# A fixed instruction order for the first two thirds of an attention and expert kernel, fp32 projections on quarters of the array, and VectorE steps over two PSUM banks

## The chip, the core and the metric

The kernel runs on one core of a Trainium2 chip. The metric is the device time of one execution in microseconds (us); lower is better. The engines are TensorE (PE in the profile, its weight loads PEld), VectorE (DVE), ScalarE (ACT), GpSimd (POOL) and SyncE (SP), whose queue issues most transfers. Each engine runs its own instructions in order and waits for the others by semaphores.

## What is computed

Three parts in a row, all in fp32 accuracy:

```python
# linear attention: 2 batches, 8 heads, 576 tokens, head size 64, 128 random features
phi(x): h = (x*scale) @ omega.T - |x*scale|^2/2;  h -= max(h);  exp(h) / sqrt(128)
kv  = sum over tokens of phi(k) v^T;  z = sum of phi(k)
x   = phi(q) kv / (phi(q) z + 1e-6)                      # 1152 tokens x 512
# gated linear part
x   = (((x @ w1) * (x @ w2)) @ w3) @ w_out               # 512 -> 1024 -> 1024 -> 512
# routed experts: 8 experts, one per token, capacity 288
e   = argmax(x @ w_gate);  gate = softmax(x @ w_gate)[e]
y   = relu(x @ e1[e]) @ e2[e];  out = gate * y for tokens within the capacity
```

The weights w1, w2, w3 and w_out come as float64.

## The kernel before

*Precision.* Most products split each fp32 operand into a high part (`F32R`, fp32 rounded for one fast pass) and a low part, and multiply in three passes, `PASS = ((0,0),(0,1),(1,0))`: high x high, high x low, low x high.

*Attention.* Tokens go in 9 tiles of 128, for k (`k0`..`k8`) and q (`q0`..`q8`). A tile is loaded as 128 partitions (two heads of 64 features) x 4 head pairs x 128 tokens. `split` (L195) casts it to high on ScalarE and takes the low part on GpSimd, or on VectorE for k0 and k2. `phi` (L202) projects, for each of two groups `g` of four heads, by 6 matmuls of 256 columns against `om_hl`, a block-diagonal omega; then VectorE takes the maximum per head (L212), and either VectorE subtracts it and ScalarE takes one exponential of 512 (L215, L216), or ScalarE takes four exponentials of 128 with the maximum as bias (L219); `SUBK` and `SUBQ` say which. `kv_add` (L238) accumulates phi(k) v into two PSUM banks, on half arrays of 64 columns. For q, `q_tr` (L221) transposes, `num` (L254) multiplies by kv, and VectorE divides (L267 to L269), `x_tr` (L272) transposes the result and splits it (L286, L287).

*Hidden layer.* `ab_mm(f, c, w)` (L425) is 12 matmuls of 288 columns for feature block f (8 of 128), token quarter c (4 of 288) and w1 or w2: 64 such groups. The product of the two goes to `g_t[f]` on VectorE (L448) or, for f 4 to 6, on GpSimd (L446). `turn` (L402) transposes 32 x 32 blocks on VectorE (L405), and `store` writes them to the table `gd` in DRAM from where the experts' tokens are gathered.

*Weights.* A block of 512 KB of float64 is loaded (L322, L344), VectorE builds fp32 in three steps on the integer words (L325 to L327, L350 to L355), ScalarE casts the high part and GpSimd takes the low part (L330/L331, L360/L364). 40 blocks: 8 each of w1, w2 and w_out, and 16 of w3. `W(f)` (L465) is w3 x w_out, 24 matmuls of 512 columns. `gate_t`, `gate_u` and `logits` (L487 to L513) make w3 w_out w_gate and the gate logits.

*Order.* The front part, up to the bar in `PLAN` (L49), is written in program order, with the order of each engine but TensorE left to the tile framework. From the bar on, `tick` (L133) hands out the pending steps of weight blocks and transposes between the matmul groups, at most one step an engine, and `keep_order` (L164) fixes the order found on VectorE, ScalarE, GpSimd and SP; `in_order(nc.tensor)` fixes TensorE's from the start. The closing part, with routing, gathers and experts, is ordered by the string `END` (L58), and the last 12 `ab_mm` groups stand in it. PSUM's eight banks are three rings: `pa` of 4, `pm` of 2, `px` of 2.

Of the kernel before, what the change touches and what calls it, by code (L numbers as in the profile page):

```python
# [28 lines left out]
AHEAD = 4  # L29
# [4 lines left out]
DVE_LOW = ("k0", "k2")  # L34

SUBK = [(0, 1), (), (0, 1), (0, 1), (), (), (), (), ()]
SUBQ = [(1,), (0, 1), (0, 1), (1,), (), (1,), (1,), (), (1,)]

KV_AT = {2: (0,), 4: (1, 2), 6: (3, 4), 8: (5, 6), 10: (7, 8)}


STEP = "PTtpANXa"

POOL_AB = [(f, b) for f in range(4, 7) for b in range(2)]

PLAN = (  # L49
# [3 lines left out]
)  # L53


# [6 lines left out]
def attention_moe_kernel(ctx: ExitStack, tc: tile.TileContext, qT, kT, v, om, w1, w2, w3, wo, wg, e1, e2, cap, out):  # L62
# [13 lines left out]
    psa = ctx.enter_context(tc.tile_pool(name="psa", bufs=4, space=bass.MemoryType.PSUM))  # L76
    psm = ctx.enter_context(tc.tile_pool(name="psm", bufs=2, space=bass.MemoryType.PSUM))

    psx = ctx.enter_context(tc.tile_pool(name="psx", bufs=2, space=bass.MemoryType.PSUM))

    def px(nm):
        return psx.tile([128, 512], F32, tag="px", name=nm)
# [28 lines left out]
    todo, active, out_of, done_of, LIM = [], [], {"wr": 0, "u": 0, "W": 0}, {}, {"wr": 2, "u": 2, "W": 2}  # L111
    late, hold, leave = [False], [False], set()
# [57 lines left out]

    zeros = wt("W", [128, 4 * (D + 1)], F16, "zeros")
    nc.gpsimd.memset(zeros, 0.0)
    om_sb = u([128, 2 * M], F32, "om_sb")
    nc.sync.dma_start(out=om_sb, in_=om)
    om_hl = wt("W", [128, 2, 2 * M], F32R, "om_hl")

    A.mul(out=om_hl[:, 0], in_=om_sb, mul=SCALE)
    V.scalar_tensor_tensor(out=om_hl[:, 1], in0=om_sb, scalar=SCALE, in1=om_hl[:, 0].bitcast(F32), op0=ALU.mult, op1=ALU.subtract)
# [4 lines left out]
    kt, qt, vt, kp, qp, qpT, kvz, kvp, xs, xhl = {}, {}, {}, {}, {}, {}, {}, {}, {}, {}  # L183

    def load(dst, src, i, nm):
        dst[i] = kq([128, 4, 128], F32, f"{nm}{i}")
        nc.sync.dma_start(out=dst[i], in_=src[i].rearrange("p (k t) -> p k t", k=4))

    def load_v(i):
        vt[i] = u([128, H, D + 1], F32, f"v{i}")  # L190
        nc.sync.dma_start(out=vt[i], in_=v[i * 128:(i + 1) * 128, :].rearrange("p (h d) -> p h d", d=D + 1))

    PASS = ((0, 0), (0, 1), (1, 0))

# [892 lines left out]
```

## Time and profile before

| | |
|---|---|
| time, median of 3 runs | 336.76 us (336.29 to 336.81) |
| the profiled execution's own time | 335.43 us |
| its span, first to last instruction | 333.6 us |
| TensorE busy | 319.7 us, 96%, 2963 matmuls |
| VectorE busy | 220.7 us, 66% |
| ScalarE busy | 145.9 us, 44% |
| GpSimd busy | 135.5 us, 41% |
| moved by the transfers | 47.77 MB |

The attention fills the first 63 us or so, the hidden layer and the W products run up to the routing near 215 us, and gathers and experts follow. Busy time of TensorE is a sum over stretches in which at least one matmul is under way; the end of a matmul is modelled, so its start is the surer number. In a timeline, a row with xN stands for N instructions in a row, its length from the first start to the last end.

### The profile page before, as it was taken

To read this page: it belongs to the slowest core of one execution; us is meant where nothing else is said; L and a number is where in the kernel's file an instruction comes from. 1 tells how busy PE (TensorE), PEld (TensorE's weight loads), DVE (VectorE), ACT (ScalarE), POOL (GpSimd) and SP (SyncE) were. 2 spreads that over 40 slices of the span, in tenths; PEclk is the share of its full clock that TensorE was granted. 3 is DMA by queue.
4 is the path that set the end of the run, shared out by engine and by line. 5 is a ranking of instruction groups with operands and counts; after the bars stand their busy time and mean duration, and the time that the engine had idled before them with its cause. 6 is when DMAs were issued, how large, how long until landed. Compare 5 with 4: busy or idle time off the path is not lost. (4 is left out here: it accounts for less than half of the span.)

```text
span 333.6 us, 7487 instructions
## 1 busy us (share of the span) xinstructions
PE 319.7 (96%) x2963; PEld 295.1 (88%) x2963; DVE 220.7 (66%) x426; ACT 145.9 (44%) x347; POOL 135.5 (41%) x118
## 2 busy tenths in 40 slices
PE   8899989999999999999999998999999999999991
PEld 6799979999998898897788896899799999899991
DVE  2979999999998944935889864380696714416110
ACT  4899898843322233243334243211553625327100
POOL 3736930133344243453575556025071633247021
PEclk9999999999999999999999999999999999999997
DMA  7986110143454728994244430994789772350011
GB/s 242 398 327 178 55 59 2 63 128 129 140 178 135 259 112 184 215 184 83 73 131 157 147 126 3 317 109 122 274 179 131 250 231 65 104 159 1 3 30 46
DMA packets 25148, 47.77 MB, mean 143 GB/s; under 512 B 3116, under 2 KB 12460, under 8 KB 25110
## 3 DMA queue, kind: packets, MB, share of 16 engines
q1 hardware_dynamic: 16950, 40.18, 39.1%
q10 hardware_dynamic: 7104, 3.54, 7.8%
q0 software_dynamic: 1056, 3.54, 3.7%
q8 instruction: 25, 0.41, 0.5%
q14 instruction: 13, 0.11, 0.1%
HBM read 38.98 MB, written 8.27 MB: 142 GB/s over the span
## 5 line engine op out<-in xcount | busy, mean ns | idle before, releaser
L433 PE MATMUL ab<-xh,w_hl 128*128 128x288 f32 x512 | 107.9, 299 | 0.8 <-ACT a_sb L437 0.6
L433 PEld LDWEIGHTS ab<-xh,w_hl 128*128 128x128 f32 x512 | 83.5, 188 | 4.0 <-issue 1.9
L433 PE MATMUL ab<-xl,w_hl 128*128 128x288 f32 x256 | 75.5, 295 | 0.0
L433 PEld LDWEIGHTS ab<-xl,w_hl 128*128 128x128 f32 x256 | 48.1, 188 | 0.0
L472 PE MATMUL W<-wo_hl,w_hl 128*128 128x512 f32 x192 | 46.3, 396 | 0.0
L472 PEld LDWEIGHTS W<-wo_hl,w_hl 128*128 128x128 f32 x192 | 35.5, 188 | 7.6
L364 POOL TENSOR_TENSOR w_hl<-w_f,w_hl 128x512 fp32r<-128x512 f32 x22 | 30.2, 1382 | 11.7 <-ACT w_hl L360 9.5
L405 DVE STREAM_TRANSPOSE gs<-g 128x576 f32<-128x576 f32 x16 | 19.7, 1232 | 15.3 <-POOL g L446 15.2
L360 ACT CAST w_hl<-w_f 128x512 fp32r<-128x512 f32 x22 | 13.7, 625 | 35.6 <-DVE w_f L355 32.1
L841 PE MATMUL r_x2p<-r_xc,W 128*128 128x288 f32 x192 | 26.8, 297 | 0.2 <-DVE r_yo L875 0.2
L350 DVE TENSOR_SCALAR w_f<-w_raw 128x512 uint32<-128x512 uint32 x22 | 17.8, 809 | 13.7 <-POOL w_hl L364 12.9
L841 PEld LDWEIGHTS r_x2p<-r_xc,W 128*128 128x128 f32 x192 | 25.8, 188 | 0.5 <-DVE r_yo L875 0.4
L331 POOL TENSOR_TENSOR wo_hl<-wo_f,wo_hl 128x512 fp32r<-128x512 f32 x8 | 11.2, 1406 | 34.1 <-PE xT L276 18.4
L480 POOL TENSOR_TENSOR W<-W_raw,W 128x512 fp32r<-128x512 f32 x8 | 10.8, 1351 | 30.9 <-ACT u_all L504 23.7
L331 POOL TENSOR_TENSOR w_hl<-w_f,w_hl 128x512 fp32r<-128x512 f32 x10 | 14.0, 1401 | 22.4 <-ACT w_hl L330 22.4
L437 ACT COPY a_sb<-ab 128x288 f32<-128x288 f32 x32 | 12.7, 398 | 21.3 <-PE ab L433 20.7
L355 DVE SCALAR_TENSOR_TENSOR w_f<-w_raw,w_f 128x512 uint32<-128x512 uint32 x22 | 20.5, 932 | 0.6
L351 DVE SCALAR_TENSOR_TENSOR w_f<-w_raw,w_f 128x512 uint32<-128x512 uint32 x22 | 18.7, 848 | 0.8
L446 POOL TENSOR_TENSOR g<-a_sb,b_sb 128x288 f32<-128x288 f32 x12 | 10.7, 888 | 18.0 <-ACT b_sb L445 15.6
L761 POOL TENSOR_TENSOR r_e_00l<-r_e_0r,r_e_00h 128x512 fp32r<-128x512 f32 x4 | 6.1, 1514 | 29.0 <-ACT r_e_00h L757 21.1
L210 PE MATMUL pjk<-om_hl,k_hl 128*128 128x256 f32 x108 | 15.2, 291 | 1.7 <-DVE kp L215 1.6
L448 DVE TENSOR_TENSOR g<-a_sb,ab 128x288 f32<-128x288 f32 x20 | 8.9, 447 | 11.9 <-PE ab L433 11.9
(233 smaller groups left out, 681.7 us busy)
## 6 DMA issues: line engine op xcount, KB each, us to landing
w_raw<-in_w SPq DMA_DIRECT2D x32, 512.0 KB, 3.6
wo_raw<-in_wo SPq DMA_DIRECT2D x8, 512.0 KB, 3.9
gd<-gs ACTq DMA_DIRECT2D x12, 288.0 KB, 7.9
v<-in_v SPq DMA_DIRECT2D x9, 260.0 KB, 5.7
k<-in_kT SPq DMA_DIRECT2D x9, 256.0 KB, 4.5
q<-in_qT SPq DMA_DIRECT2D x9, 256.0 KB, 7.1
out<-zero SPq DMA_DIRECT2D x1, 2304.0 KB
r_e_0r<-in_e SPq DMA_DIRECT2D x4, 512.0 KB
```

The source lines that it names most:

```text
L210: nc.tensor.matmul(out=ps[:, r * 256:(r + 1) * 256], lhsT=t[:, s, k * 128:(k + 1) * 128], rhs=om_hl[:, w], start=(n == 0), stop=(n == 2))
L331: nc.gpsimd.tensor_tensor(out=hl[1], in0=f.bitcast(F32), in1=hl[0].bitcast(F32), op=ALU.subtract)
L350: V.tensor_scalar(out=f, in0=r[:, :, 1], scalar1=3, scalar2=0x3FFFFFF8, op0=ALU.logical_shift_left, op1=ALU.bitwise_and)
L351: V.scalar_tensor_tensor(out=f, in0=r[:, :, 1], scalar=0xC0000000, in1=f, op0=ALU.bitwise_and, op1=ALU.bitwise_or)
L355: V.scalar_tensor_tensor(out=t["f"], in0=r[:, :, 0], scalar=29, in1=t["f"], op0=ALU.logical_shift_right, op1=ALU.bitwise_or)
L360: A.copy(out=h[:, 0], in_=t["f"].bitcast(F32))
L364: nc.gpsimd.tensor_tensor(out=h[1], in0=t["f"].bitcast(F32), in1=h[0].bitcast(F32), op=ALU.subtract)
L405: V.transpose(out=sts[b][:, :, :, f % GF], in_=g_t[f][:, b * S:(b + 1) * S].rearrange("p (j t) -> p j t", t=32))
L433: nc.tensor.matmul(out=p[:, :C], lhsT=w12[f][w][s][:, k, :], rhs=xhl[c][r][:, k], start=(n == 0), stop=(n == 11))
L437: A.copy(out=abp[f, c], in_=p[:, :C])
L472: nc.tensor.matmul(out=p, lhsT=w3_t[f, k // 4][s][:, k % 4, :], rhs=wo_t[k][r], start=(n == 0), stop=(n == 23))
L841: nc.tensor.matmul(out=p4[d][:, :C], lhsT=w_t[f][:, s, d * 128:(d + 1) * 128], rhs=xc[r][f // 4][:, f % 4], start=(f == 0 and (s, r) == (0 ...
```

## The change

- A table, `ORDER`, lists 655 words such as `PJ.k0@2`; each calls one function `t_...` that issues one step, and the number behind @ is the PSUM bank. The order of the words is the order on every engine and queue from the first instruction to the routing. `mark()` moves to the start, so `keep_order` now covers everything. The old loops, `PLAN`, `STEP`, `KV_AT` and the like go.
- q and k are projected in plain fp32. `t_PJ` issues 16 matmuls a tile, on quarters of the array: 64 partitions (one head) by 64 tokens, with 128 columns of omega. Heads of the lower partitions go to one bank, those of the upper to the next. Casts and subtractions of q, k and omega go; omega is scaled once by ScalarE.
- VectorE's maximum (`MX`), subtraction (`SUB`) and the divisions (`RD`, `X`) take both banks of a tile in one instruction: 128 x 1024 instead of 128 x 512. 12 of the 18 tiles use `SUB` with one exponential of 1024 (`EX`), the others eight exponentials of 128 (`E0`, `E1`).
- All products ahead of the routing are taken by VectorE (`G`); GpSimd keeps those of f 5 and 6 in the closing part. Two of the routing's constants are made on GpSimd.
- Weight blocks have two raw buffers (`wr`); the second ring, in the tag `W`, goes. The converted w1 and w2 of f 0 and 1 stay in tag `W`.
- Stores of the first four feature blocks, and of the last four for batch 0, are issued from SP's queue. The zero fill of the output (`ZD`) is issued from SP behind the last of them.
- PSUM is one tile of eight banks; behind the table, the rings `pm`, `px` and `pa` are dealt from the banks in the order in which they were last used.

```diff
+ORDER = """
+LDW.w10 IDENT WU@0 LDOM LD.k0 LD.k7 LD.k3 LDV.0 LDV.8 LD.k4 LD.k1 LDV.4 WA.w10 LD.q5 OMS LD.q4 WB.w10 LD.k6 PJ.k0@2 LDV.3 WC.w10 LDW.w20 LDV.7 PJ.k7@4
+CAST.w10 MX.k0 LD.k5 LDV.1 LOW.w10 PJ.k3@6 LD.q3 LD.q0 MX.k7 E0.k0 LD.k2 KO.0@0 SUB.k7 E1.k0 MX.k3 PJ.k1@4 EX.k7 LD.q6 KV.0 MX.k1 E0.k3 PJ.k4@2 SUB.k1
...
+NUM.2@4 XH.0 WC.w21 NUM.1@6 E0.q3 XL.0 LOW.w11 LDW.w22 RD.2 PJ.q5@2 X.2 E1.q3 WA.w12 XT.2@4 RD.1 TR.3.0@5 X.1 XH.2 TR.3.1@0 WB.w12 XT.1@1 QT.3.0
+PJ.q7@6 XL.2 XH.1 PJ.q4@4 QT.3.1 XL.1 CAST.w21 MX.q5 AB.0.0.0@0 LOW.w21 MX.q4 AB.0.0.1@1 ASB.0.0 SUB.q4 AB.1.0.0@0 WA.w22 EX.q4 G.0.0 MX.q7 ZM
...
+GU.2@2 TT.6.0 WTC.7 GU.5@3 LG.3 UC.2 UC.6 GU.7@1 WTC.4 LG.6 TT.7.0 UC.5 GU.4@7 LG.5 UC.4 LG.2 UC.7 ST.1.0 LG.4 WH.6 ZD WL.4 WL.6 WL.5 WL.2
+"""
...
+    def t_PJ(b, n):
+        ps, t = psum2(b), at[n]
+        at["pj", n] = ps
+        for k in range(4):
+            for g in range(2):
+                for c in (0, 64):
+                    nc.tensor.matmul(out=ps[c:c + 64, g, k * M:(k + 1) * M], lhsT=t[64 * g:64 * g + 64, k, c:c + 64],
+                                     rhs=om_s[64 * g:64 * g + 64, g * M:(g + 1) * M], start=True, stop=True)
+
+    def t_MX(b, n):
+        at["mx", n] = mx = sm.tile([128, 2, 4], F32, tag="mx", name="mx", bufs=8)
+        V.tensor_reduce(out=mx, in_=heads(at["pj", n]), axis=AX, op=ALU.max, negate=True)
...
+    def t_SUB(b, n):
+        V.tensor_tensor(out=halves_of(phi(n)), in0=heads(at["pj", n]), in1=at["mx", n].unsqueeze(3).to_broadcast([128, 2, 4, M]), op=ALU.add)
...
+    def t_WU(b):
+        for k in range(18):
+            nc.tensor.matmul(out=banks[:, b, 0:4 * (D + 1)], lhsT=zeros[:, 0:128], rhs=zeros, start=(k == 0), stop=(k == 17))
...
+    def t_X(b, i):
+        at["x", i] = x = kq([128, H, D], F32, f"x{i}")
+        V.tensor_tensor(out=halves_of(x), in0=heads(psum2(at["nu", i]), D + 1)[:, :, :, 0:D], in1=at["rd", i].to_broadcast([128, 2, 4, D]), op=ALU.mult)
...
+    def t_LDW(b, w):
+        raw_of[w] = raw = wraw.tile([128, 1024], U32, tag="wr", name=f"{w}_raw")
+        nc.sync.dma_start(out=raw, in_=from_words(w)[0])
...
+        (nc.scalar if f >= GF and b else nc.sync).dma_start(out=gd[r0:r0 + S, c0:c0 + GF * 32].rearrange("(j p) c -> p j c", p=32),
...
+    here, last = locals(), list(range(8))
+    for word_ in ORDER.split():
+        word_, b = (word_ + "@-1").split("@")[:2]
+        what, *arg = word_.split(".")
+        here["t_" + what](int(b), *arg)
```

The other words: `LD`, `LDV`, `LDW` load a q or k tile, a v tile, a weight block; `WA`, `WB`, `WC` are the three word steps of a block, `CAST` and `LOW` its high and low part; `WU` and `KO` are products of zeros that warm up and open the k-v sums, `KV` adds to these, `KVZ` copies them out; `TR` and `QT` transpose phi(q) and copy it, `NUM` is the numerator, `XT`, `XH`, `XL` transpose and split x; `AB` is a group of `ab_mm`, `ASB` its copy; `TT` and `ST` are `turn` and `store`; `W`, `WR`, `WH`, `WL`, `GT`, `WTC`, `GU`, `UC`, `LG` are the W product, its copies and the way to the gate logits.

## Rows read from the trace of the kernel before

**Rows 1.** Busy time (instructions) by stretch: PE, PEld, DVE, ACT, POOL; clock, DMA, GB/s.
```profile
0.00:70.00 70.00, 65.55 (x899) 59.96 (x900) 60.56 (x130) 58.10 (x154) 31.15 (x33) 1.00 0.48 166
70.00:215.00 145.00, 142.82 (x1225) 127.79 (x1224) 107.25 (x149) 48.67 (x107) 65.43 (x52) 1.00 0.53 149
```
**Rows 2.** TensorE's waits: for whom, us in total, times, longest us.
```profile
PE pjk L210 <- DVE kp L215: 1.6, 1, 1.6
PE u L503 <- ACT wT L494: 1.4, 1, 1.4
PE tq L226 <- ACT qpT L227: 1.4, 1, 1.4
```
**Rows 3.** TensorE's timeline in the hidden layer: start us, us, instruction.
```profile
85.30 0.29 PE L433 MATMUL ab<-xl,w_hl 128*128 128x288 f32 x1
...
85.70 0.29 PE L433 MATMUL ab<-xl,w_hl 128*128 128x288 f32 x1
```
**Rows 4.** TensorE's timeline in the attention part.
```profile
30.08 3.14 PE L210 MATMUL pjq<-om_hl,q_hl 128*128 128x256 f32 x24
...
47.20 0.96 PE L210 MATMUL pjq<-om_hl,q_hl 128*128 128x256 f32 x6
48.00 1.04 PE L226 MATMUL tq<-ident,qp 128*128 128x128 f32 x8
48.79 0.96 PE L210 MATMUL pjq<-om_hl,q_hl 128*128 128x256 f32 x6
49.67 1.15 PE L262 MATMUL nu<-kvz,qpT 128*64 128x65 f32 x32
50.76 0.66 PE L276 MATMUL xT<-ident,x 128*128 128x128 f32 x4
```
**Rows 5.** The gate logits: as a group (busy us, mean ns), and once in the timeline.
```profile
L510 PE MATMUL lgp<-g,u_all 128*8 128x288 f32 x64 | 6.6, 405 | 0.0
...
155.48 0.67 PE L510 MATMUL lgp<-g,u_all 128*8 128x288 f32 x8
```
**Rows 6.** VectorE's timeline in the attention part.
```profile
10.36 1.88 DVE L212 TENSOR_REDUCE mx<-pjk 128x4 f32<-128x512 f32 x3
...
13.65 1.27 DVE L215 TENSOR_TENSOR kp<-pjk,mx 128x512 f32<-128x512 f32 x2
...
29.71 0.42 DVE L325 TENSOR_SCALAR w_f<-w_raw 128x512 uint32<-128x512 uint32 x1
30.17 0.69 DVE L326 SCALAR_TENSOR_TENSOR w_f<-w_raw,w_f 128x512 uint32<-128x512 uint32 x1
```
**Rows 7.** VectorE's third word step as a group: busy us, mean ns, idle before.
```profile
L355 DVE SCALAR_TENSOR_TENSOR w_f<-w_raw,w_f 128x512 uint32<-128x512 uint32 x22 | 20.5, 932 | 0.6
```
**Rows 8.** TensorE's timeline at the start.
```profile
1.12 4.03 PE L231 MATMUL kv<-zeros 128*128 128x260 f16 x18 [1.12 <-POOL zeros L172]
4.85 3.59 PE L210 MATMUL pjk<-om_hl,k_hl 128*128 128x256 f32 x24
```
**Rows 9.** Busy time by stretch, as rows 1, while q, k and v are loaded.
```profile
8.00:16.00 8.00, 6.39 (x72) 5.72 (x70) 8.00 (x14) 7.08 (x18) 5.54 (x7) 1.00 1.05 397
```
**Rows 10.** ScalarE's timeline at the start: the casts of k0 and k2.
```profile
3.90 0.62 ACT L198 CAST k_hl<-k 128x512 fp32r<-128x512 f32 x1 [0.56 <-DMA k<-in_kT]
...
6.70 0.62 ACT L198 CAST k_hl<-k 128x512 fp32r<-128x512 f32 x1 [1.15 <-DMA k<-in_kT]
```
**Rows 11.** Transfers by issuing line: KB each, median us to landing.
```profile
w_raw<-in_w SPq DMA_DIRECT2D x32, 512.0 KB, 3.6
```
**Rows 12.** SP's queue around the routing: issues.
```profile
207.88 0.65 SPq L580 DMA_DIRECT2D out<-zero  x1
...
218.29 1.55 SPq L674 DMA_DIRECT2D gd<-gate  x1
```
**Rows 13.** GpSimd's timeline: the first gather.
```profile
227.86 1.11 POOL L813 DMA_INDIRECT r_xg<-gd,r_idx  x1 [5.00 <-issue]
```
**Rows 14.** TensorE's timeline: the transposes of what was gathered.
```profile
234.88 1.56 PE L825 MATMUL r_pt<-ident,r_xg 96*128 96x96 f32 x12
```

More of the change, by code (lines that the diff above doesn't have):

```diff
@@ new lines, in half, with halves_of, psum2, heads @@
+    def half(t, g):
+        return t.rearrange("p (h r) m -> p r h m", r=2)[:, g]
+    def halves_of(t):
+        return t.rearrange("p (h r) m -> p r h m", r=2)
+    def psum2(b):
+        return banks[:, b:b + 2]
+    def heads(ps, w=M):
+        return ps[:, :, 0:4 * w].rearrange("p g (h m) -> p g h m", m=w)
+    def open_group(b, n):
+        for g in range(2):
+            for k in range(n):
+                nc.tensor.matmul(out=banks[:, b + g, 0:4 * (D + 1)], lhsT=zeros[:, 0:128], rhs=zeros, start=(k == 0), stop=False)
@@ L256, in num, with t_TR, t_QT, t_NUM @@
+    def t_TR(b, i, g):
+        for h in range(4):
+            nc.tensor.transpose(out=banks[:, b, h * 128:(h + 1) * 128], in_=phi(f"q{i}")[:, 2 * h + int(g), :], identity=ident)
+        at["tq", i, g] = b
+    def t_QT(b, i, g):
+        if ("qT", i) not in at:
+            at["qT", i] = wt("qT", [128, H, 128], F32, f"qpT{i}")
+        A.copy(out=half(at["qT", i], int(g)), in_=banks[:, at["tq", i, g]].rearrange("p (h t) -> p h t", t=128))
+    def t_NUM(b, i):
+        at["nu", i] = b
         for g in range(2):
-            ps = pm(f"nu{i}_{g}")
@@ new lines, in t_TT, with t_ST, t_W @@
+    def t_TT(b, f, x):
+        turn(int(f), int(x))
+    def t_ST(b, h, x):
+        for q in range(4):
+            store(int(h) * GF + GF - 1, int(x), q)
+    def t_W(b, f, h):
+        if h == "0":
+            at["W", f] = b
+        for k in range(4 * int(h), 4 * int(h) + 4):
+            w = k4(hl_of[f"w3{f}{h}"])
+            for s, r in PASS:
+                nc.tensor.matmul(out=banks[:, at["W", f]], lhsT=w[s][:, k % 4, :], rhs=hl_of[f"wo{k}"][r],
+                                 start=(k == 0 and (s, r) == (0, 0)), stop=(k == 7 and (s, r) == (1, 0)))
@@ L501, in gate_u, with t_GU @@
+    def t_GU(b, f):
+        at["u", f] = b
         for d in range(4):
             for j in range(0, 128, 32):
[L503 to L513 removed]
@@ L546, in attention_moe_kernel, with t_UC, t_LG, t_LGM @@
-    while len(fill) > 4:
-        ab_mm(*fill.pop(0))
+                nc.tensor.matmul(out=banks[j:j + 32, b, 0:E], lhsT=wT[f][:, d, j:j + 32], rhs=wgT[:, d], start=(d == 0), stop=(d == 3))
+    def t_UC(b, f):
+        A.copy(out=u_all[:, int(f)], in_=banks[:, at["u", f], 0:E])
+    def t_LG(b, f):
+        logits(int(f), range(4) if int(f) < 5 else range(2))
+    def t_LGM(b):
+        at["lgp"] = b
+        V.memset(banks[:, b], 0.0)
+    def t_ZM(b):
+        at["zero"] = kq([128, 512], F32, "zero")
+        nc.gpsimd.memset(at["zero"], 0.0)
@@ new lines, in logits @@
+    def logits(f, cs):
+        for c in cs:
+            at["sum", c] = n = at.get(("sum", c), 0) + 1
+            nc.tensor.matmul(out=banks[c * 32:c * 32 + E, at["lgp"], 0:C], lhsT=u_all[:, f], rhs=g_t[f][:, c * C:(c + 1) * C],
+                             start=(n == 1), stop=(n == 8))
+        tick()
+    here, last = locals(), list(range(8))
[3 more added lines that the diff above has]
+        here["t_" + what](int(b), *arg)
+        for n in range(int(b), int(b) + (2 if what in ("PJ", "KO", "NUM") else 1)):
+            if n >= 0:
+                last.remove(n)
+                last.append(n)
```

632 lines of the change are left out of this document (257 added, 375 removed), and 3 rows, old and new, of the table PLAN.

## The prediction

> **What bounds the kernel now.** I read the busy shares by stretch, then TensorE's waits, then its timeline. Up to 70 us TensorE (65.55 us), VectorE (60.56) and ScalarE (58.10) are all nearly full; from 70 us to the routing at 215 TensorE is busy for 142.82 of 145 us and VectorE for 107.25 [rows 1]. A busy TensorE proves nothing alone, since the ends of pipelined matmuls are modelled, so two more views: the waits it shows are few and short, 1.6 and 1.4 us in the attention part and 1.4 us later [rows 2], and inside a group the matmuls follow one another evenly, three hidden-layer matmuls every 0.40 us [rows 3]. So TensorE's own work sets the end nearly everywhere; time comes off if it gets less to do or if its waits go. The granted clock is 1.00 in both stretches [rows 1], the 2.4 GHz level: nothing is to be won back there.
>
> **The projections, the TensorE work that changes.** Before, a q or k tile takes 12 matmuls of 256 columns. Twenty-four took 3.14 us, and six took 0.80 us from their start to the next group's [rows 4]: 1.57 to 1.60 us a tile; with 1.57, 18 tiles are 28.3 us. After, a tile has 16 fp32 matmuls of 128 columns on quarters of the array, and the trace shows each fp32 matmul as two instructions (32 gate-logit products are 64 [rows 5]), so 32 a tile. No row shows quarters of 64 rows by 64 columns. The nearest row is the gate logits, four column tiles of 32 over all 128 rows: eight instructions of 288 columns took 0.67 us together, where one alone takes 0.405 [rows 5]. So all eight started within 0.265 us, in which the hidden-layer stream starts two of 288 columns [rows 3]: four run side by side, and a round of four costs 0.265 us at most. Scaled to 128 columns a round is 0.118 us, a tile of 8 rounds 0.94, 18 tiles 17.0 us: my value. The bounds: quarters no dearer than their share of columns, 16 us; or two quarters on the same columns taking turns, 16 rounds, 1.89 us a tile, 34 us.
>
> A change of tile shape costs too. Six projections ahead of the half-array products take 0.88 us instead of 0.80, and those 32 products 1.09 us [rows 4], where 16 pairs of 65 columns at the round's pace (0.265 x 65 / 288 = 0.060 us) are 0.96: 0.21 us for a way in and out. The table has the projections in 11 separate places of TensorE's order: 2.3 us. The openings of the k-v sums grow by 0.3. Together -28.3 + 17.0 + 2.3 + 0.3 = **-8.7 us**, bounds -12 and +8.6. The Trainium skill (TensorEngine Tiling (Array Packing), Key Properties) says that a change of tiling mode drains TensorE and that tiles work independently; the 0.21 us is how large the first shows here, and no run here shows the second for quarters.
>
> **The splits that go.** 18 casts on ScalarE, 16 subtractions on GpSimd and 2 on VectorE disappear. Their cover was TensorE itself, so I price them at nothing; the way from load to projection gets shorter, and VectorE's word steps meet GpSimd less often: the same step takes 0.69 us alone and 0.932 on average [rows 6, 7].
>
> **VectorE over two banks.** Maxima or subtractions of 512 elements follow one another after 0.60 us or so (three in 1.88, two in 1.27) [rows 6]. One of 1024 I take at 1.2 us; only a fixed part, some 0.1 us, could go. Thus 18 maxima cost what 36 did, and 12 subtractions stand where 15 half as long stood: +5.4 us. The small divisor steps are halved, the triangle and rank constants go to GpSimd, and eight products come from GpSimd into a stretch where VectorE has 38 us free [rows 1]. VectorE's load hardly changes, while TensorE in front of it gets faster.
>
> **The start and the attention part.** The first weight load (512 KB) is put ahead of omega and k0 on SP's queue. k0 was cast at 3.90 us and k2 at 6.70 [rows 10]; k0 now has as many bytes up to it as k2 had, so the first projection starts between 5.5 and 6.9 us, not at 4.85 [rows 8]. From then on loads arrive at 397 GB/s [rows 9], fast enough for what is listed. VectorE starts its first maximum near 7.2 us. Ahead of the first hidden-layer product it has 13 maxima and 8 subtractions (25.2 us), 14 word steps (five of 0.42, nine of 0.69, 8.3 us) and the divisor, product and split of three tiles (4.2), 37.7 us in all, of which 1.1 lie ahead of that first maximum: the product starts no sooner than 43.8 us. TensorE has ahead of it the zeros (3.7 and 0.8), 16 projections with 10 ways in and out (17.1), k-v sums worth nine numerators (9.8), eight groups of transposes (0.4 each), three numerators (1.09 each) and 1.5 of other transposes, 39.4 us from 1.12 us on [rows 4, 8]. So it waits 3.3 us, start included, against 3.0 before [rows 2]: with something for the links between the engines **+0.5 us**, bounds -2 and +5.
>
> **Up to the routing.** By the steps listed, VectorE has 8 us or more less to do than TensorE up to the last token tile, and more from there: cover for every word step. Weights now have two raw buffers throughout, where the first ten conversions behind the front part had up to four. A refill waits for the third word step of the weight before the last, then 3.6 us of landing [rows 11] and 1.8 of steps: about 3 us a weight on two buffers. TensorE asks for 19 weights in its first 108 us and 37 in 170, so none is late on average. Four feature blocks' stores move from ScalarE's queue to SP's; the weight load behind them waits, with TensorE's cover as above. The 1.4 us wait for a gate transpose [rows 2] and smaller ones are there for the table to remove; I take 2 us off and leave 1 us for new ones: **-1.0 us**, bounds -2 and +4.
>
> **Behind it.** The closing part keeps its order, but 2.3 MB of zeros for the output now follow the last stores on SP's queue. Before, they were issued at 207.88 us, ahead of the stores, and the gate values at 218.29 [rows 12]; the first gather ran at 227.86 [rows 13], its transposes at 234.88 right behind other work [rows 14]. Now zeros stand between stores and gate: 2.3 MB at 397 GB/s are 5.8 us, of which the stores' earlier end gives some 3.5 back, so the gather comes 2 to 3 us later against the routing. Hidden-layer products cover it up to 234.88, and leave little. **+1.0 us**, bounds 0 and +3.
>
> **Sum.** -8.7 + 0.5 - 1.0 + 1.0 = -8.2 us on the profiled execution's 335.4: 327.2. The median of the runs stands 1.4 us above that execution: 328.6 us.
>
> **The rivals.**
> - *VectorE sets the pace of the attention part.* Up to the last token tile the table lists 18 maxima and 12 subtractions (36 us), 16 weights, which at 0.932 / 0.69 of the undisturbed price [rows 6, 7] take 2.4 us each (39), 18 half-microsecond steps and nine divisors (13), nine products and two transposes (6): 94 us behind a start near 6, so 100, where TensorE has 91 us of work and 4.4 of start and waits. That makes 5 us more, 333.5. For it: VectorE's busy share of 87% there [rows 1]; against it: GpSimd, which disturbs it, has 16 steps fewer. The Trainium skill (TensorEngine Tiling (Array Packing), PSUM Bottleneck) warns of this: tiling speeds up TensorE and not the emptying of PSUM.
> - *Quarters on the same columns take turns.* A tile costs 1.89 us, 17 us more in all, of which the attention part's waits (3.3) swallow a part: 342 us, slower. It decides from a round of about 0.17 us on: the gain of 8.2 us over 144 rounds is 0.057, on top of 0.118. For it: no row shows two row halves at work together; against it: column tiles run four abreast.
> - *Nearly all waits go too,* and TensorE is dense from its first projection: 323 us. Against it: the sums of the attention part above.
> - *Late weights:* two to four weights come a turn of 3 us late at the W products: 335 to 341 us.
>
> **How the numbers follow.** Forecast 0.60 (325 to 332); VectorE's pace 0.12; turns 0.12; no waits 0.10; late weights 0.06. The range 322.5 to 335.5 leaves out the turns, most of the late weights and a little on either side. A measurement of this kernel can tell about 0.2% (0.7 us) from no change. Faster: 0.60 + 0.12 + 0.10 = 0.82; slower: 0.14, the turns and some late weights; same 0.04.
>
> **What would show it.** Right: 32 projection instructions in about 0.95 us a tile; the first hidden-layer product near 44 us. Wrong: 32 in 1.8 us or more; waits of TensorE on VectorE above 6 us before 60 us; waits for w3 weights; more than 3 us idle ahead of the gather's transposes; a granted clock of 0.5 in the first 25 us, where TensorE waits for loads.

## The result

The changed kernel takes 338.89 us (median), the kernel before 336.37 us; the ratio is 1.0068, with a 95% interval of 1.0049 to 1.0086. It is slower by 0.7%, where 328.6 us was forecast. The profiled execution took 338.85 us, its span is 337.2 us (before 333.6).

The part in which the forecast's gain was to arise came out as forecast. TensorE's timeline at the start, and VectorE's maximum over two banks as a group (busy us, mean ns, idle before):

```profile
5.55 1.50 PE L250 MATMUL banks<-om_s,k 64*64 64x128 f32 x32 [0.35 <-DMA k<-in_kT]
...
11.18 1.10 PE L250 MATMUL banks<-om_s,k 64*64 64x128 f32 x32 [1.40 <-DVE k7p L263]
12.21 1.15 PE L296 MATMUL banks<-v,k0p 128*64 128x65 f32 x32
```
```profile
L255 DVE TENSOR_REDUCE mx<-banks 128x8 f32<-128x1024 f32 x18 | 21.7, 1217 | 2.5 <-PE banks L250 2.3
```

A tile takes 1.03 us from its first of 32 instructions to the next group's (11.18 to 12.21), where [rows 4] showed 1.57 to 1.60. The first hidden-layer product starts at 46.44 us instead of 63.96, but the table now takes it ahead of the last token tiles, so the two starts don't stand behind the same work. Up to 140 us the changed kernel runs as the same kernel does without the stores of the next paragraphs (0.47 us apart, `no_st2` below). Then it falls back, between 146 and 176 us. Busy time by stretch (columns as in [rows 1]):

```profile
140.00:150.00 10.00, 9.13 (x127) 7.48 (x125) 8.37 (x12) 3.46 (x9) 5.59 (x5) 1.00 1.08 191
150.00:160.00 10.00, 9.75 (x68) 8.65 (x60) 2.27 (x5) 1.35 (x3) 1.29 (x1) 1.00 1.10 201
160.00:170.00 10.00, 7.96 (x32) 6.27 (x33) 2.56 (x3) 2.08 (x5) 3.08 (x2) 0.83 1.06 140
170.00:180.00 10.00, 5.00 (x20) 4.32 (x19) 8.70 (x12) 2.91 (x7) 2.95 (x2) 0.68 0.37 123
```

VectorE, with 8 us of work in ten on either side, does 2.3 to 2.6 us in ten from 150 to 170; TensorE runs dry from 160 on, and its granted clock falls to 0.83 and 0.68 on average (0.50, the lower level of 1.2 GHz, from 176 to 180 us, behind the stop of 5.00 us shown below). The transfer engines are full (1.06 to 1.10) and yet move only 140 to 201 GB/s, where they moved 397 when they loaded q, k and v [rows 9].

Who keeps them full stands in SP's queue, its rows by time (start us, us of issuing, what, how many):

```profile
138.84 0.93 SPq L371 DMA_DIRECT2D w_raw<-in_w  x2
140.58 3.99 SPq L535 DMA_DIRECT2D gd<-gs  x4
145.09 3.03 SPq L371 DMA_DIRECT2D w_raw<-in_w  x2
148.53 8.53 SPq L535 DMA_DIRECT2D gd<-gs  x4
159.56 19.66 SPq L371 DMA_DIRECT2D w_raw<-in_w  x5
```

The stores of feature blocks 0 to 3 come in two pieces of four, 1.2 MB each. The weight loads around them landed 12.5 us (145.09 to 157.56), 12.0 (146.88 to 158.86) and 11.0 us (159.56 to 170.53) after their issue, against 3.6 in [rows 11]. What that does to VectorE, ScalarE and TensorE, in the order of the chain (timelines of each engine):

```profile
147.25 1.26 DVE L530 STREAM_TRANSPOSE gs<-g 128x576 f32<-128x576 f32 x1
157.66 0.43 DVE L378 TENSOR_SCALAR w_f<-w_raw 128x512 uint32<-128x512 uint32 x1 [9.15 <-DMA w_raw<-in_w]
...
170.62 0.43 DVE L378 TENSOR_SCALAR w_f<-w_raw 128x512 uint32<-128x512 uint32 x1 [7.99 <-DMA w_raw<-in_w]
...
175.34 0.62 ACT L389 CAST w_hl<-w_f 128x512 fp32r<-128x512 f32 x1 [2.13 <-DVE w_f L384]
175.87 0.39 ACT L405 COPY a_sb<-banks 128x288 f32<-128x288 f32 x1
...
164.31 7.00 PE L425 MATMUL banks<-wo_hl,w_hl 128*128 128x512 f32 x24 [0.44 <-ACT W L435]
176.31 0.61 PE L400 MATMUL banks<-xh,w_hl 128*128 128x288 f32 x1 [5.00 <-ACT a_sb L405]
```

Read from the bottom: TensorE stops for 5.00 us because a bank is not copied out; the copy (175.87) needs no weight at all, but in ScalarE's order it stands behind the cast of 175.34, which waits for VectorE's word steps, and these wait at 170.62, after 7.99 us of idleness, for a raw weight on its way. VectorE's waits for raw weights are the second largest sum in the view of waits (for whom, us in total, times, longest):

```profile
DVE w_f L378 <- DMA w_raw<-in_w: 31.7, 13, 9.2
...
PE banks L400 <- ACT a_sb L405: 5.0, 1, 5.0
```

The kernel before issued the same stores on ScalarE's queue, and but for the first two it issued them one at a time, with other work between (ScalarE's timeline of before):

```profile
125.22 0.90 ACTq L410 DMA_DIRECT2D gd<-gs  x2
...
129.79 0.31 ACTq L410 DMA_DIRECT2D gd<-gs  x1
...
131.61 0.31 ACTq L410 DMA_DIRECT2D gd<-gs  x1
...
140.24 0.31 ACTq L410 DMA_DIRECT2D gd<-gs  x1
```

Behind the routing a second, smaller loss stands. GpSimd's last product ahead of the gather, and the first gather (against [rows 13]); the first two lines are the changed kernel, the last two the run `zd_first` below, which issues the zeros earlier:

```profile
221.78 0.91 POOL L559 TENSOR_TENSOR g<-a_sb,b_sb 128x288 f32<-128x288 f32 x1 [2.96 <-ACT b_sb L558]
231.09 1.13 POOL L782 DMA_INDIRECT r_xg<-gd,r_idx  x1 [8.40 <-issue]
```
```profile
219.45 0.92 POOL L559 TENSOR_TENSOR g<-a_sb,b_sb 128x288 f32<-128x288 f32 x1 [2.96 <-ACT b_sb L558]
222.73 1.13 POOL L782 DMA_INDIRECT r_xg<-gd,r_idx  x1 [2.36 <-issue]
```

As a mark for the routing I take GpSimd's first product behind the gate logits. Here it is in GpSimd's timelines, in the kernel before, in the changed kernel and in `no_st2` below, which is without the stores:

```profile
218.25 0.80 POOL L446 TENSOR_TENSOR g<-a_sb,b_sb 128x288 f32<-128x288 f32 x1 [11.26 <-ACT b_sb L445]
```
```profile
218.00 0.81 POOL L559 TENSOR_TENSOR g<-a_sb,b_sb 128x288 f32<-128x288 f32 x1 [1.73 <-ACT b_sb L558]
```
```profile
205.92 0.81 POOL L562 TENSOR_TENSOR g<-a_sb,b_sb 128x288 f32<-128x288 f32 x1 [1.70 <-ACT b_sb L561]
```

So up to the routing (218.25 us before, 218.00 after) 0.25 us was won in place of 9.2, and behind it 119.20 us stand in place of 115.35: 3.85 us lost in place of 1.0. Together +3.6, which is the difference of the two spans.

### The profile page after: what moved, and what is told of

Same layout as the page of the kernel before. It is cut to its first block, busy times and chain, and to the rows that moved or that the text cites. A ratio compares the mean times of both kernels' runs of the same rounds, so it can differ in the third digit from the quotient of the medians.

```text
span 337.2 us, 8022 instructions
## 1 busy us (share of the span) xinstructions
PE 314.2 (93%) x3325; PEld 287.9 (85%) x3325; DVE 213.0 (63%) x381; ACT 128.3 (38%) x280; POOL 108.1 (32%) x96
## 5 line engine op out<-in xcount | busy, mean ns | idle before, releaser
L400 PE MATMUL banks<-xh,w_hl 128*128 128x288 f32 x416 | 90.1, 304 | 7.2 <-ACT a_sb L405 5.0
L400 PEld LDWEIGHTS banks<-xh,w_hl 128*128 128x128 f32 x416 | 69.2, 191 | 9.5 <-ACT a_sb L405 5.4
L400 PE MATMUL banks<-xl,w_hl 128*128 128x288 f32 x208 | 62.2, 299 | 0.0
L425 PE MATMUL banks<-wo_hl,w_hl 128*128 128x512 f32 x192 | 47.9, 406 | 0.5 <-ACT W L435 0.4
L425 PEld LDWEIGHTS banks<-wo_hl,w_hl 128*128 128x128 f32 x192 | 37.0, 196 | 9.2 <-ACT W L435 0.8
L400 PEld LDWEIGHTS banks<-xl,w_hl 128*128 128x128 f32 x208 | 39.8, 191 | 0.2
L378 DVE TENSOR_SCALAR w_f<-w_raw 128x512 uint32<-128x512 uint32 x32 | 15.0, 467 | 31.8 <-DMA w_raw<-in_w 31.7
L384 DVE SCALAR_TENSOR_TENSOR w_f<-w_raw,w_f 128x512 uint32<-128x512 uint32 x32 | 27.7, 868 | 0.8
L811 PE MATMUL banks<-r_xc,W 128*128 128x288 f32 x192 | 26.8, 298 | 0.2 <-DVE r_yo L847 0.2
L811 PEld LDWEIGHTS banks<-r_xc,W 128*128 128x128 f32 x192 | 25.7, 188 | 0.5 <-DVE r_yo L847 0.4
L381 DVE SCALAR_TENSOR_TENSOR w_f<-w_raw,w_f 128x512 uint32<-128x512 uint32 x32 | 24.8, 774 | 0.8
L255 DVE TENSOR_REDUCE mx<-banks 128x8 f32<-128x1024 f32 x18 | 21.7, 1217 | 2.5 <-PE banks L250 2.3
L550 PE MATMUL banks<-xh,w_hl 128*128 128x288 f32 x96 | 20.2, 301 | 0.0
L410 DVE TENSOR_TENSOR g<-a_sb,banks 128x288 f32<-128x288 f32 x26 | 11.6, 446 | 8.3 <-PE banks L400 5.0
L550 PEld LDWEIGHTS banks<-xh,w_hl 128*128 128x128 f32 x96 | 15.6, 188 | 0.6 <-issue 0.5
L550 PE MATMUL banks<-xl,w_hl 128*128 128x288 f32 x48 | 14.2, 296 | 0.0
```

What stands on the lines that cost most here:

```text
L255: V.tensor_reduce(out=mx, in_=heads(at["pj", n]), axis=AX, op=ALU.max, negate=True)
L378: V.tensor_scalar(out=f, in0=word(w, 1), scalar1=3, scalar2=0x3FFFFFF8, op0=ALU.logical_shift_left, op1=ALU.bitwise_and)
L381: V.scalar_tensor_tensor(out=words_of[w], in0=word(w, 1), scalar=0xC0000000, in1=words_of[w], op0=ALU.bitwise_and, op1=ALU.bitwise_or)
L384: V.scalar_tensor_tensor(out=words_of[w], in0=word(w, 0), scalar=29, in1=words_of[w], op0=ALU.logical_shift_right, op1=ALU.bitwise_or)
L400: nc.tensor.matmul(out=banks[:, b, :C], lhsT=hl[s][:, k, :], rhs=xhl[int(c)][r][:, k], start=(n == 0), stop=(n == 11))
L410: V.tensor_tensor(out=g_t[int(f)][:, int(c) * C:(int(c) + 1) * C], in0=abp.pop((f, c)), in1=banks[:, at["ab", f, c, "1"], :C], op=ALU.mult)
```

## The experiments

Three theories for the middle: the *queue* (a weight load waits behind the stores on SP's queue), the *packets* (stores on any queue fill the transfer engines), and the *buffers* (with two raw buffers VectorE falls behind whatever the stores do). The last was tested only from its other side, without stores; a third raw buffer was not tried. Each ratio is to the kernel before on the same chip, with its 95% interval.

**The stores back on ScalarE's queue (`st_act`).**
```diff
-        (nc.scalar if f >= GF and b else nc.sync).dma_start(...
+        (nc.sync if f >= GF and b == 0 else nc.scalar).dma_start(...
```


> The changed kernel with one edit: the stores of the first four feature blocks are issued from ScalarE's queue again, at the same place of the table. Theory Q (weight loads wait in SP's queue behind eight stores of 288 KB in 512-byte packets): the loads issued between the stores land in 4 to 6 us instead of 12.4 and 11.0, VectorE's wait for weight blocks falls from 31.7 us below 12, TensorE's 5.0 us wait near 171 us and the low clock behind it go, and the time falls by 8 to 13 us, to 326 to 331. Theory B (two raw buffers are too few, whatever the queue): the waits for weight blocks stay above 25 us, time within 2 us of 338.9. Theory D (the packets fill the transfer engines on any queue): the loads still land after 9 us or more, the time falls by less than 4 us.

335.73 us, 0.9983 [0.9955, 1.0010]: 3.2 us better than the change, level with before. The queue has a price in this pair, but it is not the main cause: VectorE still waits 25.7 us for raw weights, and TensorE still stops, for 4.5 us. On ScalarE's queue the pieces look the same, and ScalarE itself now stands behind its own stores:

```profile
152.53 5.47 ACTq L535 DMA_DIRECT2D gd<-gs  x4
158.04 0.40 ACT L405 COPY a_sb<-banks 128x288 f32<-128x288 f32 x1 [5.40 <-DMA gd<-gs]
```

The Trainium skill (DMA: Bandwidth & Descriptors, Queues, rings and completion order) says that SP's and ScalarE's queues feed the same 16 transfer engines and own none of their own; the 25.7 us agree with that.

**The stores of the kernel before on SP's queue (`before_st_sp`).**
```diff
-            (nc.sync if f >= GF and b == 0 else nc.scalar).dma_start(...
+            (nc.scalar if f >= GF and b else nc.sync).dma_start(...
```


> The kernel before with one edit: the stores of the first four feature blocks are issued from SP's queue instead of ScalarE's, where the planner puts them, one at a time between other steps. Theory Q: weight loads behind a store land in 8 us or more, TensorE waits for W products, 3 to 10 us slower than before, 339 to 346. Theory B (the raw buffers are what matters; here some weight blocks have more of them): 1 us slower at most. Theory S (four stores in one piece are what does it, not the queue): no slower by more than 2 us, since they stay spread out here.

339.62 us, 1.0129 [1.0086, 1.0173]: the kernel before, with its old projections, loses 3.7 us by this line alone. In SP's queue its last four stores draw together as well:

```profile
143.72 3.77 SPq L410 DMA_DIRECT2D gd<-gs  x4
147.53 12.20 SPq L344 DMA_DIRECT2D w_raw<-in_w  x4
```

A load issued at 149.24 us landed at 158.67. So the move that I had covered "with TensorE's cover" costs about as much in either kernel. Since the stores draw together here, this run does not part the queue from the piece of four.

**The zeros for the output right behind the last weight load (`zd_first`).**
```diff
-... ST.1.0 LG.4 WH.6 ZD WL.4 ...
+... ST.1.0 LG.4 WH.6 WL.4 ...
-... LOW.w25 LDW.w26
+... LOW.w25 LDW.w26 ZD
```


> The changed kernel with one edit: the zero fill of the output is issued right behind the last weight load, ahead of the last stores, as it was before. My step on the closing part (zeros between stores and gate values delay the first gather): TensorE's 1.5 us wait for gathered rows goes and the gaps of 0.9 and 1.2 us ahead of its transposes near 235 us with it, time 1 to 2.5 us less, 336.5 to 338. Rival (the gather waits for the stores or for its own issue): the wait stays, time the same within 0.7 us. The weight loads behind the early stores are untouched in both.

333.76 us, 0.9928 [0.9904, 0.9953]: 5.1 us better than the change, more than the 1 to 2.5 expected. The gather comes 3.3 us after the product ahead of it, not 9.3 (the lines above). Setting the starts of the same TensorE instructions of the two traces side by side, this run is 2.33 us ahead at 234.58 us and 5.43 at 245.08: the late zeros cost 3.1 us there. The other 2.3 lie between 160 and 176 us, ahead of the zeros (191.46 us), where the two kernels are the same: in this pair of traces less was lost in the middle. The change's executions reach from 336.3 to 341.8 us, those of this run only from 332.5 to 334.1; that the early zeros themselves are worth more than 3.1 us is therefore neither shown nor excluded.

**The quarters of one tile row by row (`rows_apart`, on `st_act`).**
```diff
-        for k in range(4):
-            for g in range(2):
+        for g in range(2):
+            for k in range(4):
```


> As st_act, with the two row halves of a projection apart: all 8 matmuls of the lower 64 partitions of a tile first, then those of the upper 64, so that quarters of different rows can seldom be under way together. If the quarters of two row halves run side by side in the changed kernel (0.95 to 1.0 us a tile there), a tile takes 1.7 to 1.9 us here and the first hidden-layer product starts 8 to 12 us later than in st_act. If the four abreast come from elsewhere (the columns alone), a tile stays near 1.0 us.

338.79 us in one run. Two tiles of this kernel, and one of `st_act` with the group behind it (TensorE's timelines):

```profile
14.26 3.16 PE L250 MATMUL banks<-om_s,k 64*64 64x128 f32 x64
17.35 1.15 PE L296 MATMUL banks<-v,k3p 128*64 128x65 f32 x32
```
```profile
10.67 1.10 PE L250 MATMUL banks<-om_s,k 64*64 64x128 f32 x32 [1.66 <-DVE k7p L263]
11.70 1.15 PE L296 MATMUL banks<-v,k0p 128*64 128x65 f32 x32
```

With the two row halves one after the other a tile takes 1.54 us here (17.35 less 14.26, by two), with the halves alternating 1.03. So row halves do work side by side, as the forecast had assumed without a row: two quarters at a time take 0.096 us a round, four 0.12 to 0.13. Not every tile is slowed as much: the 18 tiles take 1.00 to 1.57 us each, 24.4 us in all, against 20.3 in `st_act` (counted as in the next section). In some places where tiles follow one another, products of two tiles alternate in the trace (near 28 us), so the halves of different tiles overlap there. The expected 1.7 to 1.9 us a tile and the first hidden-layer product 8 to 12 us later did not come (49.36 us against 48.38). The single run is 3.1 us above the median of `st_act`.

**Both edits (`both`): `st_act` and `zd_first` together.**

> The changed kernel with the first half's stores on ScalarE's queue and the zeros issued some 30 us earlier. The queue alone gave 3.2 us (338.9 to 335.7), the zeros 5.1 (to 333.8). If the two losses lie in different places, the gains add: 330 to 331. If the zeros, at their earlier place, only take the time that the stores leave free on the transfers, less: 332 to 334.

333.84 us, 0.9923 [0.9898, 0.9948]. The gains don't add; the stop in the middle (from one product's start to the next 3.6 us at 170.31 us, 2.4 at 154.93) is there as before. With the zeros early the queue is worth nothing (333.84 against 333.76 in `zd_first`); why it was worth 3.2 us with the zeros late is open.

**Without the stores of the first half (`no_st`, then `no_st2`).** The routed tokens' values are not computed from feature blocks 0 to 3; zeros stand for them in DRAM, written near 56 us in `no_st`, behind the last weight load in `no_st2`.
```diff
-        for q in range(4):
+        for q in range(4 if h == "1" else 0):
```


> The changed kernel with the stores of feature blocks 0 to 3 left out (their half of the gate products in DRAM is filled with zeros near 70 us instead, in large packets; the routed tokens' values are thus not computed from those blocks). If the stores' packets, on whatever queue, keep the weights late (packets): weight loads between 140 and 170 us land in 3.5 to 5 us, VectorE's wait for raw weights falls from 31.7 to under 12 us, TensorE's 5 us stop near 170 us goes and the time is 332 to 335 with the zeros still late. If two raw buffers or VectorE's order keep them late whatever the stores do (buffers): the stop stays at 3 us or more and the time is 337 to 339.

> The changed kernel with the stores of feature blocks 0 to 3 left out as before, and the zeros that stand for them now behind the last weight load on SP's queue, near 190 us, where no weight can be late for them. The earlier try traded the stop near 170 us for one of 4.85 us at 67 us, behind its own zeros. If the stores are all that is wrong in the middle (packets): no gap over 1 us between 46 and 215 us, a granted clock of 1.00 there, and 326.5 to 328.5, the prediction's sum without late weights but with 3 us more for the late zeros. If the stops come back without stores (buffers): 331 or more.

`no_st` takes 332.19 us, 0.9877 [0.9852, 0.9902]: the middle is clean, but with its own zeros (2.4 MB at 56.30 us, ahead of a weight load) VectorE waits 5.28 us for a raw weight and TensorE stops for 4.85 us at 67 us. These zeros go in packets of 2048 bytes, so small packets are not needed to make a load late: a large piece of other bytes ahead of it does. `no_st2` doesn't have that: 326.02 us, 0.9727 [0.9689, 0.9765], 12.9 us better than the change. Its middle:

```profile
150.00:160.00 10.00, 10.00 (x69) 9.53 (x68) 7.83 (x10) 2.96 (x6) 4.16 (x4) 1.00 0.38 125
160.00:170.00 10.00, 10.00 (x52) 8.52 (x52) 7.05 (x11) 4.01 (x9) 4.39 (x3) 1.00 0.55 165
170.00:180.00 10.00, 10.00 (x52) 8.25 (x50) 8.39 (x10) 3.40 (x7) 4.00 (x4) 1.00 0.48 152
```

TensorE full, clock 1.00, with the same two raw buffers and the same table: this settles that the stores make the weights late, and that two buffers are enough without them: VectorE's waits for raw weights sum to 12.8 us here, against 31.7. It also shows that the rest of the forecast's sum held: the routing mark is at 205.92 us, 12.3 us ahead of before.

**The first piece 17 us earlier (`st_early` on the change, `best1` on `both`).**
```diff
-... TT.2.0 ASB.0.3 ...
+... TT.2.0 TT.3.0 ST.0.0 ASB.0.3 ...
-... CAST.w17 TT.3.0 W.0.1@-1 LOW.w17 TT.1.1 ST.0.0 LOW.w341 ...
+... CAST.w17 W.0.1@-1 LOW.w17 TT.1.1 LOW.w341 ...
```


> The changed kernel with one move: VectorE's last transpose of token half 0 and the four stores behind it come right behind the transpose of block 2, some 20 us earlier, still on SP's queue. If it is the two stores of 1.2 MB within 8 us of each other that make the weights late (bunching): the loads near 145 us land in under 6 us, the stop of 5 us near 170 falls under 2, 334 to 336. If each store delays the loads behind it wherever it stands (queue): the loads near 125 us land 8 to 12 us late instead, the stop moves or stays, 337 to 340.

> All three edits: stores on ScalarE's queue, the first four of them some 20 us earlier, zeros earlier. By the packets and bunching theories 328 to 330.5, which is what the sum of the prediction said without late weights and late zeros; if bunching is not the cause, as with the first two edits alone.

338.47 us, 1.0078 [1.0054, 1.0101], and 332.94, 0.9898 [0.9875, 0.9920]. The stop goes where the piece goes: TensorE stands for 4.2 us at 136 us (3.9 at 125 in `best1`). VectorE's wait in `st_early`, and ScalarE in `best1` (timelines):

```profile
137.60 0.43 DVE L378 TENSOR_SCALAR w_f<-w_raw 128x512 uint32<-128x512 uint32 x1 [7.49 <-DMA w_raw<-in_w]
```
```profile
124.64 3.77 ACTq L535 DMA_DIRECT2D gd<-gs  x4
128.45 0.40 ACT L405 COPY a_sb<-banks 128x288 f32<-128x288 f32 x1 [5.86 <-DMA gd<-gs]
```

My theory that the two pieces stand too close falls; in `st_early` one piece of four on SP's queue is enough to stop VectorE. The stop of `best1` is another: ScalarE spends 3.77 us on issuing the four stores, and the copy that TensorE waits for stands behind them. VectorE's waits for raw weights sum to only 12.9 us in `best1`, as without the stores in `no_st2` (12.8), and yet it is 6.9 us slower than that run. Of its view of waits (for whom, us in total, times, longest):

```profile
DVE w_f L378 <- DMA w_raw<-in_w: 12.9, 12, 4.3
...
ACT a_sb L405 <- DMA gd<-gs: 11.4, 2, 5.9
```

So a piece of four has two prices: late loads, and on ScalarE's queue ScalarE's own time.

**The same eight stores one at a time (`spread` on `both`, `spread_only` on `st_act`, `spread_sp` with them on SP's queue).**
```diff
-... TT.1.1 ST.0.0 LOW.w341 ... WL.0 ST.0.1 WA.w16 ...
+... TT.2.0 TT.3.0 SQ.0.0.0 ASB.0.3 ... CAST.w310 SQ.0.0.1 ... CAST.w311 SQ.0.0.2 ... CAST.w341 SQ.0.0.3
+... WL.0 SQ.0.1.0 WA.w16 ... CAST.w321 SQ.0.1.1 ... CAST.w340 SQ.0.1.2 ... CAST.w360 SQ.0.1.3
+    def t_SQ(b, h, x, q):
+        store(int(h) * GF + GF - 1, int(x), int(q))
```


> Both edits (stores on ScalarE's queue, zeros early), and the eight stores one at a time, each behind a ScalarE cast of the table, from about 122 us to about 165 us, in place of two pieces of four. If it is four stores in one piece that keep a weight load on the way for 10 us (pieces): no load over 7 us, no gap of TensorE over 1 us between 100 and 200 us, 327 to 330. If it is the stores' bytes in packets of 512 bytes, however they are spaced (bytes): the stops only move, 332 to 334.

> The eight stores one at a time on ScalarE's queue as in the run with both edits, but the zeros for the output left at their late place. Pieces: 331 to 333.5, with the zeros' price of 5 us above the run with both. Bytes: 335 to 336.5, as with ScalarE's queue alone (335.73).

> The eight stores one at a time and the zeros early, as in the run of 328.78 us, but with the stores on SP's queue, where the weight loads are. If the length of a piece is what counts (pieces), a single store ahead of a load costs it 2 to 3 us at most and the time is within 1.5 us of 328.8. If the shared queue costs the same 3 us as with pieces of four (queue: 338.9 against 335.7): 331.5 or more.

`spread` 328.78 us, 0.9800 [0.9755, 0.9844]; `spread_only` 330.92, 0.9852 [0.9824, 0.9879]; `spread_sp` 328.25, 0.9769 [0.9744, 0.9794]. The same bytes in the same packets, 5.1 us faster than `both` (4.1 by the ratios): it is the piece, that is, how closely the stores follow one another. That they also start some 18 us sooner doesn't explain it, since `best1` starts as early. The loads beside single stores land in 3.5 to 6.6 us, as far as the trace shows their landing. A gap of 2.2 us near 147 us is left, where none over 1 us was expected. The queue no longer matters: 328.25 on SP's against 328.78 on ScalarE's. The late zeros cost 2.1 us here (330.92 less 328.78), where 5 were expected.

**Other places for the single stores (`spread2`, `spread3`).**
```diff
-... CAST.w311 SQ.0.0.2 ... CAST.w341 SQ.0.0.3 ... WL.0 SQ.0.1.0 ... CAST.w321 SQ.0.1.1 ... CAST.w340 SQ.0.1.2 ... CAST.w360 SQ.0.1.3
+... WTC.1 SQ.0.0.2 ... CAST.w321 SQ.0.0.3 ... CAST.w340 SQ.0.1.0 ... CAST.w360 SQ.0.1.1 ... CAST.w351 SQ.0.1.2 ... CAST.w330 SQ.0.1.3
```


> Stores one at a time on ScalarE's queue, zeros early, but two stores of the first half later (near 147 and 151 us instead of 132 and 136) and those of the second half from about 154 to 170 us. If what is left of the loss (some 4.9 us up to the routing against the run without stores) comes from single stores that meet the loads VectorE needs next, between 128 and 150 us: no gap over 1 us at 144 to 147, 324.5 to 327.5. If any store costs the same wherever it stands: 328 to 330.

> What the run before this was meant to be: stores one at a time on ScalarE's queue, two of the first half later (near 145 and 150 us), those of the second half from about 152 to 168 us, zeros early. The run before still had the piece of four near 151 us beside the single ones (the second half was stored twice), and its stop came back at 168 us. If single stores that meet the loads VectorE needs next between 128 and 150 us make up the rest: no gap over 1 us at 144 to 147, 324.5 to 327.5. If any store costs the same wherever it stands: 328 to 330.

In `spread2` the piece `ST.0.1` was left in the table beside the single stores, so that the second half is stored twice: 332.38 us, 0.9914 [0.9891, 0.9938], with a stop of 4.4 us at 167.83. It doesn't tell what it was made for, but shows once more what a piece does. `spread3` is without it: 327.78 us, 0.9765 [0.9743, 0.9786], the fastest of the runs that compute everything, 2.3% faster than before. Its middle:

```profile
150.00:160.00 10.00, 9.99 (x92) 8.78 (x83) 7.30 (x9) 1.83 (x5) 5.46 (x4) 1.00 0.74 202
160.00:170.00 10.00, 9.50 (x51) 7.96 (x50) 6.51 (x9) 4.61 (x9) 4.03 (x3) 1.00 0.74 186
170.00:180.00 10.00, 10.00 (x50) 8.26 (x49) 5.94 (x11) 3.83 (x7) 3.11 (x3) 1.00 0.78 202
```

The transfer engines are at 0.74 to 0.78 with the same GB/s as in the pieces (186 to 202), and the clock stays at 1.00. The gap of 2.2 us near 147 us of `spread` is 0.7 here, and gaps of 0.9 and 1.1 us come in at 167 and 186. Its routing mark, 209.33 us, is still 3.4 behind the kernel without stores: single stores are cheap, not free. The median lies between the two expected ranges and only 1.0 us below that of `spread`, with runs that overlap (326.9 to 328.0 against 327.6 to 330.3), so the places alone are not shown to decide.

**The first weight load behind k3 (`start`, on `both`).**
```diff
-LDW.w10 IDENT WU@0 LDOM LD.k0 LD.k7 LD.k3 ...
+IDENT WU@0 LDOM LD.k0 LD.k7 LD.k3 LDW.w10 ...
```


> Both edits, and the first weight load behind omega, k0, k7 and k3 on SP's queue instead of ahead of them. If the 512 KB ahead of k0 hold the first projection back: it starts 1 us or more sooner than 5.5 us, and the time is 0.5 to 1.2 us below that with both edits alone (333.84 in another call). If VectorE's first maxima or the later loads set the pace there: no difference over 0.5 us.

335.56 us, 1.0004 [0.9981, 1.0027], 1.7 us slower than `both` (2.7 by the ratios), which neither expectation allowed for. The first projection starts sooner, at 5.13 us, but VectorE's three steps on that weight stand ahead of its first maximum in the table, and now start at 7.16 us instead of 4.34; the fourth projection waits 3.95 us for it. The load at the head is there for VectorE's order; the table's DMA words can't be moved without the steps behind them.

## Why the prediction was wrong, and where it was right

**Projections (forecast -8.7): right, and a little better.** Adding up the time from each projection instruction's start to the next TensorE start, each counted with 0.5 us at most, 576 instructions take 19.7 us in the change; 17.0 and 2.3 for the ways in and out were forecast. On the side of before the same count gives 30.3 us for 216 products where I had put 28.3: the tiles I took from [rows 4] are among the faster ones. So -10.6, or -10.3 with the 0.3 of the openings, which came as forecast. The rival "turns" is out: round of four 0.12 to 0.13 us against its 0.17.

**VectorE over two banks: right.** 1217 ns against 1.2 us.

**Start and attention part (+0.5): low, inside its bounds.** The first projection at 5.55 us lies within 5.5 to 6.9. The first hidden-layer product was to come "no sooner than 43.8" and came at 46.44; TensorE is busy for 41.35 of these, where I had added up 39.4, and from its first instruction at 1.12 us on it stands for 4.0 us and not 3.3, with one stop of 1.0 us that no engine of the table caused (below). The rival of VectorE's pace is out as well: from 46 us on TensorE is dense up to 148 us.

**Up to the routing (-1.0): this is the step that failed.** I wrote that the weight load behind the four stores waits "with TensorE's cover as above". The cover I meant was VectorE's 8 us of slack; but VectorE's slack is work left over, not weights in stock. With two raw buffers and an order fixed for every engine it can be two weights ahead of the transfers and no more, and its in-order queue holds the products, transposes and, by way of the casts, ScalarE's copies that free PSUM behind the next word step. A load that lands 12 us after its issue in place of 3.6 uses that up within one turn. Missed in the diff was the form, more than the queue: `t_ST` issues four stores at once, where the kernel before issued one and did other work between. I had put the rival "late weights" at 0.06 and "two to four weights a turn of 3 us late", with 335 to 341 us: its mechanism and its time (338.9) are what came, with three loads 7 to 9 us late in place of 3; its chance was wrong. Waits for w3 weights, two of the three late loads (`w340`, `w360`), were also among my signs of being wrong. By the traces it cost 12.1 us (routing mark 218.00 against 205.92 without the stores), against a bound of +4 for the whole term. From each start to the next the same 816 hidden-layer and W products take 142.0 us in place of 130.4, 11.6 more: 6.4 of these are two gaps in which TensorE is idle (5.00 and 1.36), the other 5.2 shorter gaps and a slower pace, with the granted clock down.

Without the stores the three terms that were to give -9.2 gave -12.3. Of the 3.1 us more, the projections are 1.6; the 288 numerator products take 9.1 us instead of 10.35 and the 192 W products 44.9 instead of 45.8, which I had not priced, against the longer stops at the start.

**Behind it (+1.0): right in mechanism, too small.** 3.85 us measured, beyond the bound of +3, of which the zeros are 3.1 in one pair of traces (2.1 us by the medians of the spread pair). I let the products of the hidden layer cover the gather up to 234.88; they ran out, TensorE waited 1.5 us for the gathered rows in the change, and its clock was granted at 0.95 to 0.96 from 220 to 260 us, where the kernel before had 1.00.

**What the forecast comes to.** The sum without the two losses holds: the change with its stores one at a time and its zeros early takes 327.8 to 328.8 us, where 328.6 was forecast. That agreement is partly luck, since the projections gave more and single stores still cost 3.4 us.

## What to carry to other kernels

When a change rewrites the order of the work, read the transfers in it as closely as the instructions: how many are issued in one piece, how many bytes that is, on whose queue, and which load stands next. An engine's spare time covers a late transfer only as far as there are buffers loaded ahead of it; behind an in-order queue the wait reaches work that needs no transfer at all. And where a sum predicts a gain and the time shows none, run the kernel without the suspected transfer: one such run separated 12 us of loss from 12 us of gain.

## What the runs showed of the hardware

- **Small packets fill the transfer engines without moving much.** The stores go out in packets of 512 bytes; between 140 and 158 us one took 31 ns in the median (16.5 bytes per ns), one of 4096 bytes 159 ns (25.8). That is not for being a store: the zeros of `zd_first`, stores too, took 88 ns per packet of 2048 bytes (23.3). In the pieces the engines were at 1.08 to 1.10 for 191 to 201 GB/s; the same kernel without the stores needed 0.38 to 0.55 for 125 to 165 GB/s. The Trainium skill (DMA: Bandwidth & Descriptors, Specifications) gives 512 bytes as enough for the full rate; these rows say that it isn't here, with 397 GB/s at 1.05 for the large packets of q, k and v [rows 9]. No run sends the same stores in larger packets, so what the packet size alone costs this kernel is not shown.
- **TensorE stops at fixed instructions near 21 and 25 us.** Counting the recorded loads and products each, TensorE stands ahead of record 698 or 952 or both, 254 records apart, in the middle of a group, idle for 0.40 to 1.65 us, and the profile names no releaser. That is so in every profile of the table's kernels but `rows_apart`. Which of the two is long changes from run to run. The transfer engines are full at the first place (1.01 to 1.04 from 19 to 21 us), but so they are in `rows_apart` (1.03), and at the second the loads are just ending (from 24 to 26 us 0.29 in `best1` and 0.27 in `spread`). Here is the second one of `best1` in TensorE's timeline, with the stretch around it, and that of `spread`, the same instructions:

```profile
25.69 1.67 PE L296 MATMUL banks<-v,k7p 128*64 128x65 f32 x27 [1.50 <-issue]
27.29 1.99 PE L250 MATMUL banks<-om_s,q 64*64 64x128 f32 x32
```
```profile
24.00:28.00 4.00, 2.50 (x46) 2.30 (x46) 1.80 (x3) 2.85 (x5) 0.80 (x1) 0.73 0.39 117
```
```profile
25.41 1.03 PE L296 MATMUL banks<-v,k7p 128*64 128x65 f32 x27 [0.67 <-issue]
26.38 1.10 PE L250 MATMUL banks<-om_s,q 64*64 64x128 f32 x32
```

  Behind the stop of 1.50 us the products take twice as long and the granted clock is 0.73 over the stretch; behind that of 0.67 us they don't. The first hidden-layer product starts at 48.45 us in the one and at 46.66 in the other; executions of one kernel lie 1 to 5.5 us apart, and how much of that these stops make is not shown. The Trainium skill (Runtime: NRT & Kernel Launch, Instruction fetch mechanics) says that instructions are fetched in blocks of 256 by transfers of their own, at a cost that is mostly hidden; 254 records is close to that, since some records can be missing. The traces bear it out in time as well. They have a queue of instruction packets, of 16 KB each (queue and kind: packets, MB, share, from the page of the changed kernel):

```profile
q8 instruction: 28, 0.46, 0.6%
```

  In the 15 profiles of the table's kernels every stop of 0.4 us or more at these two products ends 1.27 to 1.60 us after the end of such a packet. In `rows_apart`, which doesn't stop, they start 1.54 and 1.67 us after one. No run changes the fetch itself, so that TensorE waits for it rests on this agreement.
